# A sparse-attention and feed-forward kernel: the local heads' scores and values brought into one visit a tile, and the x tile split in two buffers

## The chip, the cores and the metric

The kernel runs on one core of a Trainium2 chip. The metric is the device time of one execution in microseconds (us); the runs of one kernel are summed up by their median. The engines are named as the profile names them: PE is the tensor engine (PEld its loading of weights), DVE the vector engine, ACT the scalar engine, POOL the GpSimd engine, SP the engine that issues DMA transfers.

## What is computed

q, k and v have 8 batches, 8 heads, 576 positions and 64 channels. Four heads of each batch are local (a query sees the 32 positions up to itself), four are strided (a query sees the earlier positions of its own residue modulo 32). The attention's output, 4608 tokens of 512 channels, goes through a feed-forward layer with an exact gelu, 512 to 2048 to 512.

```python
rel = pos[:, None] - pos[None, :]
mask_local = (rel >= 0) & (rel < stride)
mask_strided = (rel >= 0) & (pos[None, :] % stride == pos[:, None] % stride)
scores = np.where(masks[None], scale * np.matmul(q, k.transpose(0, 1, 3, 2)), -1e9)
attn = softmax(scores)                      # max taken off, 1e-9 added to the sum
x = np.matmul(attn, v).transpose(0, 2, 1, 3).reshape(B * S, H * D)
h = x @ w_in
out = (0.5 * h * (1.0 + erf(h / sqrt(2)))) @ w_out
```

## The kernel before

**The feed-forward part** sets the frame. The 4608 tokens are cut into 12 tiles of TT = 384, the 2048 hidden channels into NF = 16 blocks of 128: 192 steps, n = 16 t + f. A float32 product is made of three products of shorter floats (high with high, low with high, high with low), so every matrix is kept as a high and a low part. Step n holds, on PE, the group H(n) (`ffn_h`: 4 chunks of 128 channels x 3 products = 12 matmuls of 384 columns, L602 to L604, into one of two H banks), then the group O(n-2) (`ffn_o`: 3 blocks of 128 tokens x 3 products = 9 matmuls of 512 columns, L641 to L643). Between them ACT makes the gelu in the bank (L611) and its high part gh (L613), and DVE takes the difference gl (L615), the last to read the bank; `ffn_o` needs both. The bank of H(n) is written again by H(n+2).

**The x tile** of a token tile t is what the H groups read: high and low part, four chunks of 128 channels by 384 tokens each (`x_tile`, two tiles alive). Chunks 0 and 1 are local heads, 2 and 3 strided ones. Whoever fills it copies the high part on ACT (L230) and subtracts for the low part on DVE (L232), by `to_x`.

**Strided heads** run on DVE alone, off PE, but for the first tile: products of q and k with a sum (L477, a multiply with a reduction and the reading of its accumulator), an exponential on ACT (L487), multiply-adds with v (L517 for the first, L519 for the rest), a transpose (L527), then `to_x`. They are spread over the steps by a running cost (`run_strided`).

**Local heads** come as 36 jobs of P = 128 tokens, three to a tile (JPT = 3). A job (`band_job`) has seven parts, separated by `yield`: part 0 the scores on PE (L290, 32 matmuls of 64 columns in two banks S0 and S1, which the three jobs of a tile share, 128 columns each), part 1 mask and maximum on DVE (L304), part 2 the exponentials on ACT (L308), part 3 normalising and transposing on DVE (L311 to L314) and DMA transfers of the result into a banded buffer, part 4 the values on PE (L328, 16 matmuls of 64 columns), parts 5 and 6 `to_x`. The jobs of tiles 0 and 1 run in the kernel's start, a list of jobs written out by hand (START), which also holds steps 0 to 15. From tile 2 on, `visit(n)` puts the parts 0 of a tile's three jobs at step 16 (t-1) + 2 and their parts 4 at step 16 (t-1) + 12, each in front of that step's H group; `softmaxes(n)` places the parts between.

**Order.** ACT's and PE's instructions stand in the order in which the program is written (`manual_schedule`); from step 16 on DVE, SP and POOL are ordered by the framework's scheduler. In the start all but POOL are in the written order. In names such as H_140, gl_140 or O_8_2 the number is the step, or the tile and its token block; X_L27 is the bank of job 27's values.

## Time and profile before

| | us |
|---|---|
| median of three runs | 885.03 (884.91 to 885.48) |
| the profiled execution | 885.1 |
| its span in the trace | 883.2 |
| PE busy | 858.5 (97%) |
| DVE busy | 716.7 (81%) |
| ACT busy | 492.7 (56%) |

The span runs from the first to the last instruction; 1.9 us of the profiled execution lie around it. The busy times are shares of a span that holds a start (some 110 us, in which weights are split and the first jobs run) and a long steady part; what a wait costs has to be read in its own place. In the timeline each line is a run of like instructions with its start and duration; matmuls are pipelined, so one starts before the end of the one ahead, and the distance of two starts is what counts.

### The profile page before, as it was taken

To read this page: it belongs to the slowest core of one execution; us is meant where nothing else is said; L and a number is where in the kernel's file an instruction comes from. 1 tells how busy PE (TensorE), PEld (TensorE's weight loads), DVE (VectorE), ACT (ScalarE), POOL (GpSimd) and SP (SyncE) were. 2 spreads that over 40 slices of the span, in tenths; PEclk is the share of its full clock that TensorE was granted. 3 is DMA by queue.
4 is the path that set the end of the run, shared out by engine and by line. 5 is a ranking of instruction groups with operands and counts; after the bars stand their busy time and mean duration, and the time that the engine had idled before them with its cause. 6 is when DMAs were issued, how large, how long until landed. Compare 5 with 4: busy or idle time off the path is not lost.

```text
span 883.2 us, 19381 instructions
## 1 busy us (share of the span) xinstructions
PE 858.5 (97%) x5984; PEld 769.2 (87%) x5984; DVE 716.7 (81%) x4897; ACT 492.7 (56%) x1003; POOL 17.9 (2%) x89
## 2 busy tenths in 40 slices
PE   4599999999999999999999999999999999999998
PEld 3488899989989889889898988998988998989997
DVE  5999999988898998898999978998789897752111
ACT  5999576358447347357636536636642743643222
POOL 5000100000000000000000000000000000000000
PEclk7599999999999999999999999999999999999999
DMA  9981420230220122112113022113012102000001
GB/s 304 348 350 56 149 82 15 86 102 23 85 81 14 62 69 77 36 42 75 58 32 109 18 75 82 21 55 127 17 57 82 49 25 63 11 11 1 36 1 36
DMA packets 34551, 66.66 MB, mean 75 GB/s; under 512 B 6800, under 2 KB 16528, under 8 KB 32400
## 3 DMA queue, kind: packets, MB, share of 16 engines
q1 hardware_dynamic: 34448, 65.43, 22.7%
q8 instruction: 47, 0.77, 0.4%
q14 instruction: 56, 0.46, 0.2%
HBM read 51.64 MB, written 9.44 MB: 69 GB/s over the span
## 4 chain that ended last, share of the span: by engine, by line
PE 93%; DVE 3%; DMA 2%; SPq 1%; issue 1%; ACT 1%; DVEq 0%
PE H L602 15%; PE O L642 15%; PE O L643 15%; PE H L604 15%; PE H L603 15%; PE O L641 15%; PE X_L L328 2%; DMA vl<-in_vl_dram 2%; PE S_L L290 1%; DVE ws L153 1%; DVE w L163 1%; DVE ws L155 1%; ACT ws L151 0%; SPq L132 0%; DVE xl L424 0%
## 5 line engine op out<-in xcount | busy, mean ns | idle before, releaser
L611 ACT ACTIVATE H<-H 128x384 f32<-128x384 f32 x192 | 91.5, 477 | 334.6 <-PE H L604 295.6
L602 PE MATMUL H<-xh,w 128*128 128x384 f32 x768 | 262.4, 342 | 2.6 <-ACT xh L230 1.2
L604 PE MATMUL H<-xh,w 128*128 128x384 f32 x768 | 260.3, 339 | 1.6 <-DVE w L163 1.6
L603 PE MATMUL H<-xl,w 128*128 128x384 f32 x768 | 259.2, 338 | 0.2 <-DVE xl L232 0.2
L519 DVE SCALAR_TENSOR_TENSOR acc<-sv,sc,acc 128x64 f32<-128x64 f32 x1158 | 250.2, 281 | 0.6
L643 PE MATMUL O<-w,gl 128*128 128x512 f32 x576 | 227.9, 396 | 0.0
L642 PE MATMUL O<-w,gh 128*128 128x512 f32 x576 | 227.5, 395 | 0.0
L641 PE MATMUL O<-w,gh 128*128 128x512 f32 x576 | 224.2, 389 | 0.0
L477 DVE CUSTOM_DVE_ANT_0 junk<-sq,sk 128x64 f32<-128x64 f32 x1290 | 206.2, 221 | 1.8 <-DMA sk<-in_ks_dram 1.8
L615 DVE TENSOR_TENSOR gl<-H,gh 128x384 fp32r<-128x384 f32 x192 | 106.3, 554 | 107.8 <-ACT gh L613 107.4
L602 PEld LDWEIGHTS H<-xh,w 128*128 128x128 f32 x768 | 145.2, 189 | 12.5 <-ACT xh L230 1.4
L603 PEld LDWEIGHTS H<-xl,w 128*128 128x128 f32 x768 | 145.1, 189 | 7.9 <-DVE xl L232 0.6
L604 PEld LDWEIGHTS H<-xh,w 128*128 128x128 f32 x768 | 145.0, 189 | 2.0 <-DVE w L163 1.9
L643 PEld LDWEIGHTS O<-w,gl 128*128 128x128 f32 x576 | 108.0, 187 | 23.0
L642 PEld LDWEIGHTS O<-w,gh 128*128 128x128 f32 x576 | 108.0, 187 | 18.2
L641 PEld LDWEIGHTS O<-w,gh 128*128 128x128 f32 x576 | 108.2, 188 | 17.4
L477 DVE DVE_READ_ACCUMULATOR2_ANT sc<- 128x1 f32 x1290 | 109.3, 85 | 0.0
L613 ACT CAST gh<-H 128x384 fp32r<-128x384 f32 x192 | 92.3, 481 | 6.0
L611 ACT ACT_TABLE_LOAD x61 | 78.3, 1283 | 1.1
L487 ACT ACT_TABLE_LOAD x35 | 44.9, 1283 | 0.6
L308 ACT ACTIVATE PT_L<-P_L,nm_L 128x64 f32<-128x64 f32 x132 | 44.3, 336 | 0.3
L308 ACT ACT_TABLE_LOAD x25 | 32.1, 1283 | 2.7 <-DMA band<-PT_L 2.2
(106 smaller groups left out, 512.0 us busy)
## 6 DMA issues: line engine op xcount, KB each, us to landing
ws<-in_w_dram SPq DMA_DIRECT2D x16, 1024.0 KB, 11.4
qk<-in_qk_dram SPq DMA_DIRECT2D x36, 320.0 KB, 4.7
out_dram<-ob SPq DMA_DIRECT2D x34, 256.0 KB, 2.5
vl<-in_vl_dram SPq DMA_DIRECT2D x36, 192.0 KB, 3.4
sk<-in_ks_dram SPq DMA_DIRECT2D x8, 576.0 KB, 4.9
sv<-in_vs_dram SPq DMA_DIRECT2D x8, 576.0 KB, 3.7
band<-PT_L SPq DMA_DIRECT2D x240, 16.0 KB, 1.8
sq<-in_qs_dram SPq DMA_DIRECT2D x4, 576.0 KB, 3.8
```

Source lines behind the costliest of these rows:

```text
L308: nc.scalar.activation(pv[:, :, h, :], p1[:, h * 2 * QB:(h + 1) * 2 * QB].rearrange("p (c t) -> p c t", c=2), AF.Exp, bias=nm[:, h:h + 1], ...
L477: nc.vector.tensor_tensor_reduce(junk, sq[vi, "q"][:, r0 + r, :], sq[vi, "k"][:, c, :], 1.0, 0.0, ALU.mult, ALU.add, ss[u][:, r, c:c + 1])
L519: nc.vector.scalar_tensor_tensor(acc[:, r, :], sq[vi, "v"][:, c, :], wgt, acc[:, r, :], ALU.mult, ALU.add)
L602: nc.tensor.matmul(hp, w1[f][:, 0, c, :], xh[:, c, :], start=(c == 0), stop=False)
L603: nc.tensor.matmul(hp, w1[f][:, 0, c, :], xl[:, c, :], start=False, stop=False)
L604: nc.tensor.matmul(hp, w1[f][:, 1, c, :], xh[:, c, :], start=False, stop=(c == NC - 1))
L611: nc.scalar.activation(hp, hp, AF.Gelu)
L613: nc.scalar.copy(gh, hp)
L615: nc.vector.tensor_tensor(gl, hp, gh.bitcast(F32), ALU.subtract)
L641: nc.tensor.matmul(o, gh[:, sl], w2[f][:, 0, :], start=(f == 0), stop=False)
L642: nc.tensor.matmul(o, gh[:, sl], w2[f][:, 1, :], start=False, stop=False)
L643: nc.tensor.matmul(o, gl[:, sl], w2[f][:, 0, :], start=False, stop=(f == NF - 1))
```

## The change

- The x tile is two tiles: the local chunks as [128, 3 jobs, 2 chunks, 128 tokens], the strided ones as [128, 2 chunks, 384 tokens]. `ffn_h` reads a local chunk in three pieces of 128 columns, one for each job; the bank that it writes stays one run of 384.
- The values of tile t and the scores of tile t+1 stand in one visit, at step 16 (t-1) + 13 for t = 2 to 11; the scores of tile 2 alone stand at step 18. That makes 11 visits: one of scores, nine of both, one of values.
- Parts 1, 2 and 3 of job i lie 1, 2 and 3 steps behind the visit plus 4 i (2 i for tile 2); before, part 1 of all three jobs lay in the visit's step, and parts 2 and 3 one and two steps behind it plus 2 i.
- The values of jobs 0 and 1 stand side by side in bank X and go into x by one `to_x` of 512 columns; job 2's go into the last 128 columns of the banks S0 and S1 that the next tile's scores take, and leave by two `to_x` of 128.
- The load of the next q and k (`load_jq`) is issued behind part 0 instead of behind part 6.

The diff:

```diff
--- before.py
+++ after.py
@@ -168,8 +168,10 @@
     xt = {}
 
     def x_tile(t):
+
         if t not in xt:
-            xt[t] = [xpool.tile([P, NC, TT], F32R, name=f"x{i}_{t}", tag=f"x{i}{t % 2}") for i in "hl"]
+            xt[t] = ([xpool.tile([P, JPT, N2, P], F32R, name=f"x{i}_{t}", tag=f"x{i}{t % 2}") for i in "hl"],
+                     [xpool.tile([P, NC - N2, TT], F32R, name=f"xs{i}_{t}", tag=f"xs{i}{t % 2}") for i in "hl"])
         return xt[t]
 
 
@@ -266,9 +268,11 @@
         if x >= JPT:
             load_jv(x + 3)
         yield
-        t, c0 = divmod(x * P, TT)
-        dst = [a[:, 0:N2, c0:c0 + P] for a in x_tile(t)]
+        dst = [d[:, x % JPT] for d in x_tile(x // JPT)[0]]
         yield from to_x(*dst, xv)
+
+    def score_banks(t):
+        return [ps_a.tile([P, DM], F32, name=f"S{j}_{t}", tag=f"S{j}") for j in range(2)]
 
     def band_job(x, bt, sx=None):
 
@@ -276,10 +280,8 @@
 
         QB = STRIDE
         i = x % JPT if sx is not None else 0
-        sx = {} if sx is None else sx
-        if i == 0:
-            sx["s"] = [ps_a.tile([P, DM], F32, name=f"S{j}_L{x}", tag=f"S{j}") for j in range(2)]
-        s = [t[:, i * P:(i + 1) * P] for t in sx["s"]]
+        sx = {x // JPT: score_banks(x // JPT)} if sx is None else sx
+        s = [t[:, i * P:(i + 1) * P] for t in sx[x // JPT]]
         qv = jq[x][:, 0:2 * N2 * LU].rearrange("p (r a t) -> p r a t", r=N2, a=2)
         kv = jq.pop(x)[:, 2 * N2 * LU:].rearrange("p (r a t) -> p r a t", r=N2, a=2)
         head = [(h % 2, slice(h // 2 * 2 * QB, (h // 2 + 1) * 2 * QB)) for h in range(HL)]
@@ -318,21 +320,34 @@
                 kb = g % 2 + c
                 nc.sync.dma_start(bt[kb * QB:(kb + 1) * QB, g, :], tv[g * QB:(g + 1) * QB, c, :])
         yield
-        if i % 2 == 0:
-            sx["x"] = ps_a.tile([P, DM], F32, name=f"X_L{x}", tag="X" if i == 0 else "S0")
-        xv = sx["x"][:, i % 2 * N2 * P:(i % 2 + 1) * N2 * P].rearrange("p (r q) -> p r q", r=N2)
+        if i == 0:
+            sx["x"] = ps_a.tile([P, DM], F32, name=f"X_L{x}", tag="X")
+
+        xv = [sx["x"][:, (N2 * i + r) * P:(N2 * i + r + 1) * P] if i < 2 else sx[x // JPT + 1][r][:, JPT * P:]
+              for r in range(N2)]
         bv = bt.rearrange("p (a b) (h q) -> p a b h q", a=2, h=HL)
         for r in range(N2):
             for a in range(2):
                 for j in range(2):
-                    nc.tensor.matmul(xv[rows(j), r, a * LU:(a + 1) * LU], jv[x][:, a, 2 * r + j, :],
+                    nc.tensor.matmul(xv[r][rows(j), a * LU:(a + 1) * LU], jv[x][:, a, 2 * r + j, :],
                                      bv[:LK, a, :, 2 * r + j, :], start=True, stop=True)
         jv.pop(x)
         load_jv(x + 3)
         yield
-        t, c0 = divmod(x * P, TT)
-        dst = [d[:, 0:N2, c0:c0 + P] for d in x_tile(t)]
-        yield from to_x(*dst, xv)
+        dst = x_tile(x // JPT)[0]
+        k = x % JPT
+        if i == 0 and sx.get("two"):
+            parts = []
+        elif i == 2:
+            parts = [to_x(*[d[:, k, r] for d in dst], xv[r]) for r in range(N2)]
+        else:
+            parts = [to_x(*[d[:, k - i:k + 1].rearrange("p i r q -> p (i r q)") for d in dst],
+                          sx["x"][:, 0:(i + 1) * N2 * P])]
+        for p in parts:
+            next(p)
+        yield
+        for p in parts:
+            next(p, None)
 
 
     ka = {}
@@ -413,7 +428,7 @@
                         nc.tensor.matmul(xv[b][h * 32:(h + 1) * 32, c, :], pts[kr, c, h * 32:h * 32 + 32],
                                          vv[kr, c, h, :], start=True, stop=True, tile_position=(b * 32, h * 32))
             yield
-        xd = [x[:, N2:].rearrange("p e (m c b) -> b p c e m", c=NGR // 4, b=4) for x in x_tile(t)]
+        xd = [x.rearrange("p e (m c b) -> b p c e m", c=NGR // 4, b=4) for x in x_tile(t)[1]]
         for b in range(4):
             nc.vector.transpose(xs[:, b].rearrange("p c e m -> p (c e m)"), xv[b].rearrange("p c d -> p (c d)"))
         yield
@@ -528,8 +543,8 @@
                                 acc.rearrange("p t d -> p (t d)"))
 
             def split():
-                dst = [x[:, N2:N2 + DH, 32 * k:32 * (k + nr)].rearrange("p e (t r) -> p e t r", r=32)
-                       for x in x_tile(t)]
+                dst = [x[:, :, 32 * k:32 * (k + nr)].rearrange("p e (t r) -> p e t r", r=32)
+                       for x in x_tile(t)[1]]
                 return to_x(*dst, xs.rearrange("p t e r -> p e t r"))
             splits.append((t, split, u))
         ops.append((0.6, fin))
@@ -596,12 +611,16 @@
 
     def ffn_h(n):
         t, f = divmod(n, NF)
-        xh, xl = xt[t]
+        loc, strided_ = xt[t]
         hp = ps_h.tile([P, TT], F32, name=f"H_{n}", tag="H")
         for c in range(NC):
-            nc.tensor.matmul(hp, w1[f][:, 0, c, :], xh[:, c, :], start=(c == 0), stop=False)
-            nc.tensor.matmul(hp, w1[f][:, 0, c, :], xl[:, c, :], start=False, stop=False)
-            nc.tensor.matmul(hp, w1[f][:, 1, c, :], xh[:, c, :], start=False, stop=(c == NC - 1))
+            if c < N2:
+                o, (xh, xl) = hp.rearrange("p (i q) -> p i q", i=JPT), [x[:, :, c, :] for x in loc]
+            else:
+                o, (xh, xl) = hp, [x[:, c - N2, :] for x in strided_]
+            nc.tensor.matmul(o, w1[f][:, 0, c, :], xh, start=(c == 0), stop=False)
+            nc.tensor.matmul(o, w1[f][:, 0, c, :], xl, start=False, stop=False)
+            nc.tensor.matmul(o, w1[f][:, 1, c, :], xh, start=False, stop=(c == NC - 1))
         hps[n] = hp
 
     def ffn_g(n):
@@ -768,10 +787,15 @@
 
 
 
-    SCORES, VALUES = 2, 12
-    score_at = {ready[t - 1] + SCORES: t for t in range(2, NTILE)}
-    value_at = {ready[t - 1] + VALUES: t for t in range(2, NTILE)}
-    banks = {}
+    FIRST, VISIT = 2, 13
+    value_at = {ready[t - 1] + VISIT: t for t in range(2, NTILE)}
+    score_at = {ready[1] + FIRST: 2, **{n: t + 1 for n, t in value_at.items()}}
+    soft_at = {}
+    for n, t in score_at.items():
+        for i in range(JPT):
+            for p in (1, 2, 3):
+                soft_at.setdefault(n + p + i * (2 if t == 2 else 4), []).append((t * JPT + i, p))
+    banks = {"two": True}
     local = {}
     band = slot("band", [P, 4 * DM])
     nc.gpsimd.memset(band, 0.0)
@@ -785,28 +809,30 @@
                 local[x] = [band_job(x, bts[x % NBT], banks), 0]
             assert local[x][1] == p
             local[x][1] += 1
-            if next(local[x][0], True) is not None:
+            next(local[x][0], None)
+            if p == 0:
                 load_jq(x + 3)
 
     def visit(n):
 
-        for at, p in ((score_at, 0), (value_at, 4)):
-            for i in range(JPT if n in at else 0):
-                part(at[n] * JPT + i, p)
+        t = value_at.get(n, 0)
+        if n in score_at:
+            banks[score_at[n]] = score_banks(score_at[n])
+        for i in range(JPT if t else 0):
+            part(t * JPT + i, 4)
+        for i in range(JPT if score_at.get(n, NTILE) < NTILE else 0):
+            part(score_at[n] * JPT + i, 0)
 
     def softmaxes(n):
 
-        for i in range(JPT if n in value_at else 0):
-            part(value_at[n] * JPT + i, 5, 6)
-        for i in range(JPT if n in score_at else 0):
-            part(score_at[n] * JPT + i, 1)
-        for i in range(JPT):
-            for d, p in ((1, 2), (2, 3)):
-                t = score_at.get(n - 2 * i - d)
-                if t is not None:
-                    if p == 2:
-                        flush_exps(NU)
-                    part(t * JPT + i, p)
+        t = value_at.get(n, 0)
+        for i in range(JPT if t else 0):
+            part(t * JPT + i, 5, 6)
+        for x, p in soft_at.get(n, ()):
+            if x < NJ:
+                if p == 2:
+                    flush_exps(NU)
+                part(x, p)
 
     def step(n):
 
```

On PE, the value visit of tile 9 (jobs 27 to 29), before: between O(137) and H(140) there stand values alone.

```order
L642 MATMUL O_8_2_9117<-w_9_1000,gh_137_9538 128x512
L643 MATMUL O_8_2_9117<-w_9_1000,gl_137_9539 128x512
L328 MATMUL X_L27_9694<-band_1485,vl_27_8597 64x64 x8
L328 MATMUL X_L27_9694<-band_1485,vl_28_8607 64x64 x8
L328 MATMUL X_L29_9715<-band_1485,vl_29_8618 64x64 x8
L602 MATMUL H_140_9726<-xh_8_7858,w_12_1084 128x384
L603 MATMUL H_140_9726<-xl_8_7859,w_12_1084 128x384
```

The scores of tile 10 (jobs 30 to 32) end six steps on, in front of H(146):

```order
L290 MATMUL S0_L30_10057<-qk_32_9754 32x64
L290 MATMUL S1_L30_10058<-qk_32_9754 32x64
L602 MATMUL H_146_10107<-xh_9_8882,w_2_644 128x384
L603 MATMUL H_146_10107<-xl_9_8883,w_2_644 128x384
L604 MATMUL H_146_10107<-xh_9_8882,w_2_644 128x384
```

After, the same values stand one step later, in front of H(141), and the scores follow on them (96 instructions, of which the first two are shown; the last is followed by H(141)):

```order
L662 MATMUL O_8_2_9143<-w_10_760,gl_138_9601 128x512
L332 MATMUL X_L27_9758<-band_1489,vl_27_8678 64x64 x8
L332 MATMUL X_L27_9758<-band_1489,vl_28_8688 64x64 x8
L332 MATMUL S0_10_9756<-band_1489,vl_29_8698 64x64 x4
L332 MATMUL S1_10_9757<-band_1489,vl_29_8698 64x64 x4
L292 MATMUL S0_10_9756<-qk_30_8716 32x64
L292 MATMUL S1_10_9757<-qk_30_8716 32x64
```

In front of H(146) nothing is left but the step's own groups:

```order
L661 MATMUL O_8_2_9143<-w_15_1188,gh_143_9955 128x512
L662 MATMUL O_8_2_9143<-w_15_1188,gl_143_9956 128x512
L621 MATMUL H_146_10152<-xh_9_8962,w_2_646 128x384
L622 MATMUL H_146_10152<-xl_9_8963,w_2_646 128x384
L623 MATMUL H_146_10152<-xh_9_8962,w_2_646 128x384
```

The values went from step 140 to 141 and the scores from 146 to 141, job 29's values into S0 and S1.

On DVE, the place of the subtractions of job 29 and of gl_141, before. acc and xs belong to unit 33 of the strided heads, z and sc to unit 34, junk to unit 36:

```order
L519 SCALAR_TENSOR_TENSOR acc_33_9679<-sv_9_8656,sc_33_9217,acc_33_9679 128x64
L232 TENSOR_TENSOR xl_9_8883<-X_L29_9715,xh_9_8882 128x2x128
L503 TENSOR_REDUCE z_34_120<-sc_34_9589 128x4
L519 SCALAR_TENSOR_TENSOR acc_33_9679<-sv_9_8656,sc_33_9217,acc_33_9679 128x64
L509 TENSOR_SCALAR z_34_120<-z_34_120 128x4
L527 STREAM_TRANSPOSE xs_33_9926<-acc_33_9679 128x256
L510 RECIPROCAL z_34_120<-z_34_120 128x4
L477 ISA junk_36_0_0_10272,sc_36_10270<-sq_10_9496,sk_10_9498 128x64
L477 ISA sc_36_10270 128x1
L477 ISA junk_36_1_0_10274,sc_36_10270<-sq_10_9496,sk_10_9498 128x64
L477 ISA sc_36_10270 128x1
L615 TENSOR_TENSOR gl_141_9795<-H_141_9781,gh_141_9794 128x384
```

After, behind gl_140; the gl that follows is gl_141, behind 31 pairs of junk and sc, of which the first stands here, and four first products and four multiply-adds among these:

```order
L634 TENSOR_TENSOR gl_140_9727<-H_140_9713,gh_140_9726 128x384
L534 SCALAR_TENSOR_TENSOR acc_33_9698<-sv_9_8630,sc_33_9243,acc_33_9698 128x64
L518 TENSOR_REDUCE z_34_120<-sc_34_9608 128x4
L534 SCALAR_TENSOR_TENSOR acc_33_9698<-sv_9_8630,sc_33_9243,acc_33_9698 128x64 x4
L524 TENSOR_SCALAR z_34_120<-z_34_120 128x4
L534 SCALAR_TENSOR_TENSOR acc_33_9698<-sv_9_8630,sc_33_9243,acc_33_9698 128x64 x4
L525 RECIPROCAL z_34_120<-z_34_120 128x4
L534 SCALAR_TENSOR_TENSOR acc_33_9698<-sv_9_8630,sc_33_9243,acc_33_9698 128x64 x3
L522 TENSOR_TENSOR sc_34_9608<-sc_34_9608,z_34_120 128x4x8
L534 SCALAR_TENSOR_TENSOR acc_33_9698<-sv_9_8630,sc_33_9243,acc_33_9698 128x64 x5
L542 STREAM_TRANSPOSE xs_33_10019<-acc_33_9698 128x256
L492 ISA junk_36_0_0_10299,sc_36_10297<-sq_10_9515,sk_10_9517 128x64
```

The subtractions of the local heads moved behind gl_141, and work of the strided heads that stood behind gl_141 moved ahead of it.

## Rows read from the trace of the kernel before

**Rows 1.** The page, parts 1 and 2: busy time; granted clock of PE in 40 slices.

```profile
...
PE 858.5 (97%) x5984; PEld 769.2 (87%) x5984; DVE 716.7 (81%) x4897; ACT 492.7 (56%) x1003; POOL 17.9 (2%) x89
...
PEclk7599999999999999999999999999999999999999
...
```

**Rows 2.** Waits of PE: engine, line, releaser; us in total, times, longest.

```profile
...
PE H L602 <- DVE gl L615: 0.3, 1, 0.3
...
```

**Rows 3.** Timeline of PE, a step without a visit; start, duration, instruction.

```profile
...
303.07 0.39 PE L641 MATMUL O<-w,gh 128*128 128x512 f32 x1
...
304.92 0.39 PE L643 MATMUL O<-w,gl 128*128 128x512 f32 x1
305.15 0.33 PE L602 MATMUL H<-xh,w 128*128 128x384 f32 x1
305.32 0.34 PE L603 MATMUL H<-xl,w 128*128 128x384 f32 x1
...
307.26 0.39 PE L641 MATMUL O<-w,gh 128*128 128x512 f32 x1
...
```

**Rows 4.** Timeline of PE at the value visit of step 60.

```profile
...
298.99 0.40 PE L643 MATMUL O<-w,gl 128*128 128x512 f32 x1
299.31 1.62 PE L328 MATMUL X_L<-band,vl 96*64 96x64 f32 x48
300.86 0.44 PE L602 MATMUL H<-xh,w 128*128 128x384 f32 x1
301.14 0.33 PE L603 MATMUL H<-xl,w 128*128 128x384 f32 x1
...
```

**Rows 5.** Timeline of PE at the score visit of step 66.

```profile
...
325.85 0.40 PE L643 MATMUL O<-w,gl 128*128 128x512 f32 x1
326.18 1.17 PE L290 MATMUL S_L<-qk 64*32 64x64 f32 x96
...
327.56 0.34 PE L603 MATMUL H<-xl,w 128*128 128x384 f32 x1
...
```

**Rows 6.** Timeline of PE in the start, values followed by scores.

```profile
...
53.39 1.01 PE L328 MATMUL X_L<-first,vl 96*64 96x64 f32 x16
54.34 0.46 PE L290 MATMUL S_L<-qk 64*32 64x64 f32 x32
...
```

**Rows 7.** Timeline of PE, last matmul of H(139) and H(140), first of H(142).

```profile
...
647.25 0.33 PE L604 MATMUL H<-xh,w 128*128 128x384 f32 x1
...
653.18 0.33 PE L604 MATMUL H<-xh,w 128*128 128x384 f32 x1
...
659.62 0.33 PE L602 MATMUL H<-xh,w 128*128 128x384 f32 x1
...
```

**Rows 8.** Timeline of DVE around steps 138 to 141.

```profile
...
642.79 0.74 DVE L517 TENSOR_SCALAR acc<-sv,sc 128x64 f32<-128x64 f32 x4
...
649.60 0.54 DVE L615 TENSOR_TENSOR gl<-H,gh 128x384 fp32r<-128x384 f32 x1
...
650.46 4.98 DVE L519 SCALAR_TENSOR_TENSOR acc<-sv,sc,acc 128x64 f32<-128x64 f32 x25
655.37 0.54 DVE L615 TENSOR_TENSOR gl<-H,gh 128x384 fp32r<-128x384 f32 x1
...
659.10 0.45 DVE L527 STREAM_TRANSPOSE xs<-acc 128x256 f32<-128x256 f32 x1
...
```

**Rows 9.** Timeline of DVE around steps 91 to 93.

```profile
...
443.91 0.23 DVE L477 CUSTOM_DVE_ANT_0 junk<-sq,sk 128x64 f32<-128x64 f32 x1 [1.60 <-DMA sk<-in_ks_dram]
...
444.06 0.22 DVE L477 CUSTOM_DVE_ANT_0 junk<-sq,sk 128x64 f32<-128x64 f32 x1
...
452.98 0.56 DVE L615 TENSOR_TENSOR gl<-H,gh 128x384 fp32r<-128x384 f32 x1
...
```

**Rows 10.** Timeline of PE, first matmul of H(95).

```profile
...
453.70 0.34 PE L602 MATMUL H<-xh,w 128*128 128x384 f32 x1
...
```

**Rows 11.** Waits of DVE, columns as in rows 2.

```profile
...
DVE gl L615 <- ACT gh L613: 107.4, 45, 5.4
...
```

## The prediction

> **What bounds the kernel now.** I read the page first, then the waits of the tensor engine (PE), then its timeline around the visits of the local heads, and last the vector engine's (DVE) timeline. [...] The list of PE's waits has twelve rows; eleven name operations of the start or its first tiles, and the one on the step's last operation, gl, is 0.3 us in all [rows 2]; it lies at 55 us, in the start too. After the start PE waits for nothing: a step without a visit takes 4.19 us, 303.07 to 307.26, and inside it the way from the last matmul of an O group (L643) to the second matmul of the next H group (L603) takes 0.40 us [rows 3]. That 0.40 is the unbroken passage against which I price a visit.
>
> A **value visit** (48 matmuls, L328) stands in that passage and stretches it from 298.99 to 301.14, 2.15 us: it costs 1.75 [rows 4]. A **score visit** (96 matmuls, L290) stretches it from 325.85 to 327.56, 1.71 us: 1.31 [rows 5]. Ten tiles pay both: 10 x 3.06 = 30.6 us. The ends of a visit are the part that a merge can save: 0.32 us pass between the start of the last L643 and that of the visit's first matmul (298.99 to 299.31), where unbroken the next matmul comes after 0.23 (304.92 to 305.15), and on the way out the first H matmul holds the second up for 0.28 (300.86 to 301.14) instead of 0.17. That is about 0.2 us a visit; the rest is the matmuls themselves, which stay.
>
> **The change, part by part.** *Merging.* Values of tile t and scores of t+1 now stand in one visit: nine merged ones (steps 29, 45, ..., 157), one of scores alone (18) and one of values alone (173): 11 visits for 20. I build a merged one from rows: 0.32 entry; 1.55 of values, from L328's start to the start of what follows (299.31 to 300.86) [rows 4]; then scores from their start to the first L603, 1.38 (326.18 to 327.56) [rows 5]; less 0.40: 2.85. The open piece is the step from values to scores, which do not adjoin in the steady part of this trace. They do once in the start: there L328 starts at 53.39 and lasts 1.01, and L290 starts at 54.34, 0.06 before that modelled end [rows 6]; H after L328 starts 0.07 before it as well (300.86 against 299.31 + 1.62) [rows 4]. So going from values to scores costs what going from values to H cost, and my sum stands: 3.06 - 2.85 = 0.20 saved, x 9 = **1.8 us**. Its bounds: nothing, if the inner step costs as much as both ends saved (nearest row against it: rows 6), and 9 x 0.32 = 2.9, if the whole entry goes. I take 1.8, since rows 6 show the very sequence.
>
> *The x tile in two buffers.* The six matmuls of each H group that read local heads now take the moving operand in three pieces of 128 columns that lie 256 apart; the result stays one run. 6 x 192 = 1152 matmuls, all on the path. No H matmul before reads pieces, but L328 does: its moving operand is two pieces of 32. 48 of them, 24 pairs of 2 x 64 columns, take 1.55 us, 65 ns a pair with the way out of the visit in it [rows 4]; an H matmul of 384 columns takes 0.17 (305.15 to 305.32) [rows 3], that is 57 ns for 128. What is over, 8 ns a pair, bounds what its four pieces cost; three pieces then cost 6 ns at most, 6.9 us in all. The other bound is nothing: I see no row that excludes it, and none that shows a gain from pieces. I take nothing, because the 24 x 8 = 0.19 us over are of the size of a visit's way out (0.1 us on the first H matmul alone).
>
> *Softmax parts moved.* Parts 1 to 3 of job i now lie 1 to 3 steps, plus 4 i, behind the visit; they are ACT and DVE work and no PE. Work is the same in number. The last bands are written some eleven steps after their visit, and PE reads them five steps on, over 20 us, far more than a band's DMA takes. *Copies.* Two jobs' values leave bank X by one ACT copy and one DVE subtraction of 512 columns, the third's by two of 128: three subtractions as before. They run beside H and O. *qk loads* are issued behind the visit instead of at the job's end; they are needed one tile, 70 us, later; on SP's queue they stand ahead of stores and bands that nobody awaits within four steps. *Banks.* S0 and S1 now hold job 2's values beside the next scores; both are read within some ten steps and written again after sixteen. All four at nothing; the cover is the whole steps in between, and where it were gone a wait of some microseconds would show on PE before L328, L290 or L602.
>
> *Order on DVE.* This is where something is given back. PE may start H(n+2) only when gl(n) has read the bank of H(n). I call the lag of n the time from the last matmul end of H(n) to the end of gl(n). With H(140) ending at 653.18 + 0.33 = 653.51 and H(142) starting at 659.62, the lag allowed is 6.11 [rows 7]. Seen: gl(139) ends 2.56 after its H (650.14 against 647.58), gl(140) 2.40 (655.91 against 653.51) [rows 7, 8]. The worst in the steady part that I found: some steps after a wait of 1.60 us for a DMA, gl(93) ended at 453.54 [rows 9], 0.16 before the H(95) that needed it [rows 10], a lag of 5.95. Forty-five of the 192 gl waited for ACT, so DVE had caught up there [rows 11]. The scheduler has now put more DVE work ahead of the gl of a merged visit's step. For step 141 I price its list: 21 multiply-adds at 0.196 (25 from 650.46 to 655.37), four first products and a transpose and gl at their rows less the 0.07 by which the next instruction starts early, 0.67 + 0.38 + 0.47 [rows 8], 31 reduce pairs at just under 0.15 (443.91 to 444.06) [rows 9], four small ones at some 0.14 (an estimate, below the shortest of these): 10.7 us, where PE needs 4.19 + 2.85 = 7.04 from H(140) to H(141). gl(140) has 3.8 us of work in 4.19, so its lag falls from 2.56 to 2.2; gl(141) comes to 2.2 + 10.7 - 7.0 = 5.9, and gl(142), with 4.8 of work in 4.19, to 6.5: 0.4 us over, which PE waits. Priced likewise, the nine visits' steps have 8.6, 8.9, 8.4, 7.7, 7.7, 7.9, 9.7, 10.7 and 9.0 us. From lags of 2.4 to 4 most end at 3 to 5.5, and only 30 and 142 come near the limit. I take **0.4 us** in all; the bounds are 0, and, if each visit were met with some 4.5 us of lag, halfway from rows 8 to rows 10, 0.4 to 1 us at eight or nine places, up to some 6 us.
>
> **Sum.** -1.8 + 0.4 = -1.4. The profiled execution took 885.1 us, of which 883.2 are span; the median of the runs is 885.03, the same within 0.1. 885.03 - 1.4 gives **883.6**. Two tenths of a per cent, 1.77 us, is about what a measurement here tells from no change; faster then means below 883.26, slower above 886.80.
>
> **Rivals.** *DVE becomes the bound at the merged visits.* For it: 81% busy [rows 1], the longer lists above, the 0.16 of rows 10. Against it: the 45 waits for ACT [rows 11]. Paid are 0.9 to 6 us, 884.1 to 889. It ends on the slower side from 1.8 + 1.77 = 3.6 us of waiting on, 0.4 us at each of nine visits, which takes lags some 2 us above that of step 140 where the visits begin.
>
> *H pays for three pieces.* From 3.1 ns for each of 1152 matmuls the kernel is slower by 0.2%: -1.4 + 3.6 = +2.2 (887.2); at 1.2 ns the gain is gone. For it: no H matmul here has read pieces, and they are all on the path. Against it: L328's pieces of 32 run near the rate of plain columns [rows 4]. [...]
>
> *The merge gives nothing,* since a visit's ends are paid between values and scores as well: 885.0 + 0.4 = 885.4; rows 6 speak against it. *The merge gives the whole entry:* 885.03 - 2.9 + 0.4 = 882.5.
>
> **How the numbers follow.** Forecast (the merge gains 1.8, give or take 0.4, DVE and pieces take 0 to 0.9; 882.8 to 884.2): 0.65, some two fifths of it below 883.26. DVE as the bound: 0.17, a quarter of it slower. Pieces: 0.08, most of it slower. Nothing from the merge: 0.05. The whole entry: 0.05, faster. Faster 0.27 + 0.05 = 0.32; slower 0.04 + 0.07 = 0.11, with 0.02 for what I have not seen 0.13; the same 0.55. The range runs from 882.4 to 886.2: the forecast, both cases of the merge, and DVE's part up to 3 us.
>
> **What would show it.** Right: the passage from L643 through a merged visit to L603 takes about 3.25 us at nine places, L290 starts just before L328's modelled end; a step without a visit still takes 4.19; PE's waits gain at most a row on gl of some tenths, near step 142. Wrong: a step without a visit of 4.205 or more (pieces: six a step at 3 ns), a row of several us on gl (DVE), a gap of over 0.2 us between L328 and L290 (no merge gain), or PE waiting before L328 or L290 for a band, a load or a bank.

## The result and the profile after

The changed kernel takes 886.72 us in the median of 20 runs, beside 885.00 for the kernel before in as many: a ratio of 1.0023, with a 95% interval of 1.0014 to 1.0031 (the ratios in this document lie nearer that of the means than that of the medians; the medians differ by 1.7 us, the means by 2.0). It is 0.2% slower, just short of what I had called slower (from 886.80 on). What the median doesn't say is the spread: 885.19 to 889.55 us, where the kernel before keeps to 884.88 to 885.68. The profiled execution is one of its shorter ones, 885.84 us with a span of 883.9.

The page of that execution, parts 1, 2 and 4. PE's busy time is the same as in [rows 1] but for 0.4 us. The third row gives each engine's share of the chain that ended last; DVE now holds 10% of it, where it held 3% (the fourth row, of the kernel before). These 10% are not time lost: where PE waits for a gl, the chain goes back through DVE's whole list in front of it, and only PE's wait at its end is paid.

```profile
...
PE 858.9 (97%) x5984; PEld 771.0 (87%) x5984; DVE 716.2 (81%) x4897; ACT 489.6 (55%) x1001; POOL 17.8 (2%) x89
...
PEclk9999999999999999999999999999999999999999
...
PE 85%; DVE 10%; DMA 2%; issue 1%; POOL 1%; ACT 1%; SPq 0%; POOLq 0%; DVEq 0%; ACTq 0%
...
```

```profile
...
PE 93%; DVE 3%; DMA 2%; SPq 1%; issue 1%; ACT 1%; DVEq 0%
...
```

**What was forecast on PE came.** Its timeline at the merged visit of step 141, from the last matmul of the O group to the second of the H group:

```profile
...
652.32 0.40 PE L662 MATMUL O<-w,gl 128*128 128x512 f32 x1
652.65 1.15 PE L332 MATMUL X_L<-band,vl 96*64 96x64 f32 x32
653.63 0.64 PE L332 MATMUL S<-band,vl 96*64 96x64 f32 x16
654.19 1.17 PE L292 MATMUL S<-qk 64*32 64x64 f32 x96
655.29 0.45 PE L621 MATMUL H<-xh,w 128*128 128x384 f32 x1
655.58 0.34 PE L622 MATMUL H<-xl,w 128*128 128x384 f32 x1
...
```

652.32 to 655.58 is 3.26 us, against the 3.25 put together from [rows 4, 5]; L292 starts 0.08 before the modelled end of L332, as in [rows 6]. Steps without a visit take 4.19 us as in [rows 3]; here are the O groups of two of them (672.39 to 676.58):

```profile
...
672.39 0.39 PE L660 MATMUL O<-w,gh 128*128 128x512 f32 x1
...
676.58 0.39 PE L660 MATMUL O<-w,gh 128*128 128x512 f32 x1
...
```

So the merge saves what it should, and matmuls that read three pieces cost nothing that can be seen.

**What took it back** stands in the waits of PE, where [rows 2] had 0.3 us:

```profile
...
PE H L621 <- DVE gl L634: 2.0, 3, 1.5
...
```

The row counts three waits, of which the longest is 1.5 us. With the time that PE's weight loads waited, the H groups behind steps 30, 141 and 142 start some 2.8 us late in sum (from last matmul to last matmul the distances are 4.65, 5.92 and 4.79 us instead of 4.19). The span grew by 0.7 us, so some 2.1 us must have been gained, near the 1.8 of the sum. The waits of DVE tell why gl came late; the columns are those of [rows 11]. First the kernel before, where PE waited for none of this, then the changed kernel:

```profile
...
DVE junk L477 <- DMA sk<-in_ks_dram: 1.8, 2, 1.6
...
DVE acc L517 <- DMA sv<-in_vs_dram: 0.9, 1, 0.9
...
```

```profile
...
DVE gl L634 <- ACT gh L632: 107.0, 45, 5.0
...
DVE junk L492 <- DMA sk<-in_ks_dram: 2.6, 2, 2.2
DVE acc L532 <- DMA sv<-in_vs_dram: 2.1, 2, 1.5
...
```

The longest wait for sk, 2.18 us, stands in front of gl(29), and PE loses some 0.5 us behind step 30; the longest for sv stands in front of gl(141), and PE loses 2.3 us behind steps 141 and 142.

In detail, at step 141. The timeline of PE gives the end of H(141), 657.66, and the start of the H(143) that waited:

```profile
...
657.32 0.34 PE L623 MATMUL H<-xsh,w 128*128 128x384 f32 x1
...
665.41 0.44 PE L621 MATMUL H<-xh,w 128*128 128x384 f32 x1 [1.49 <-DVE gl L634]
...
```

and that of DVE gives the instruction which held up everything behind it, among these gl(141):

```profile
...
662.20 0.74 DVE L532 TENSOR_SCALAR acc<-sv,sc 128x64 f32<-128x64 f32 x4 [1.48 <-DMA sv<-in_vs_dram]
...
664.80 0.56 DVE L634 TENSOR_TENSOR gl<-H,gh 128x384 fp32r<-128x384 f32 x1
...
```

gl(141) ends 7.70 us after H(141), not the forecast 5.9: DVE stood for 1.48 us in front of L532, the first product with v of a new group of the strided heads, until the load of sv had landed. That buffer has one copy, so its load starts when the old group's last product is done; it was issued at 656.94, and DVE had come to the new group's first product at 660.72, 3.8 us later. SP's timeline shows in what company the load starts:

```profile
...
653.37 1.29 SPq L191 DMA_DIRECT2D vl<-in_vl_dram  x3
654.77 0.84 SPq L185 DMA_DIRECT2D qk<-in_qk_dram  x2
656.94 0.33 SPq L469 DMA_DIRECT2D sv<-in_vs_dram  x1
657.36 0.38 SPq L185 DMA_DIRECT2D qk<-in_qk_dram  x1
...
```

Five loads of the local jobs were issued in the 3.6 us ahead of it and one right after. In the kernel before, sv is issued in the same step; the vl loads lie 8.8 us ahead of it, and the qk loads 18 us behind:

```profile
...
650.33 1.28 SPq L189 DMA_DIRECT2D vl<-in_vl_dram  x3
659.09 0.35 SPq L454 DMA_DIRECT2D sv<-in_vs_dram  x1
...
677.23 0.40 SPq L183 DMA_DIRECT2D qk<-in_qk_dram  x1
...
```

The DMA view of the 11 us around it, first of the changed kernel, then of the kernel before (the issue's last column is the median time from issue to landing): 2.19 MB move where 0.61 moved, and the same 576 KB take 5.2 us instead of 3.6.

```profile
...
DMA packets 914, 2.19 MB, mean 199 GB/s; under 512 B 112, under 2 KB 112, under 8 KB 912
...
sv<-in_vs_dram SPq DMA_DIRECT2D x1, 576.0 KB, 5.2
...
```

```profile
...
DMA packets 146, 0.61 MB, mean 56 GB/s; under 512 B 16, under 2 KB 16, under 8 KB 144
...
sv<-in_vs_dram SPq DMA_DIRECT2D x1, 576.0 KB, 3.6
...
```

### The profile page after: what moved, and what is told of

The parts are those of the page before. It is cut to its first block, busy times and chain, and to the rows that moved or that the text cites. A ratio compares the mean times of both kernels' runs of the same rounds, so it can differ in the third digit from the quotient of the medians.

```text
span 883.9 us, 19396 instructions
## 1 busy us (share of the span) xinstructions
PE 858.9 (97%) x5984; PEld 771.0 (87%) x5984; DVE 716.2 (81%) x4897; ACT 489.6 (55%) x1001; POOL 17.8 (2%) x89
## 4 chain that ended last, share of the span: by engine, by line
PE 85%; DVE 10%; DMA 2%; issue 1%; POOL 1%; ACT 1%; SPq 0%; POOLq 0%; DVEq 0%; ACTq 0%
PE H L621 14%; PE H L623 14%; PE O L661 14%; PE H L622 14%; PE O L662 14%; PE O L660 13%; DVE junk L492 2%; DVE acc L534 2%; PE X_L L332 1%; PE S L292 1%; DVE gl L634 1%; DMA sk<-in_ks_dram 1%; DVE ws L153 1%; DMA sv<-in_vs_dram 1%; DVE P_L L306 0%
## 5 line engine op out<-in xcount | busy, mean ns | idle before, releaser
L534 DVE SCALAR_TENSOR_TENSOR acc<-sv,sc,acc 128x64 f32<-128x64 f32 x1158 | 254.2, 286 | 0.6
L621 PE MATMUL H<-xh,w 128*128 128x384 f32 x384 | 133.1, 347 | 4.3 <-DVE gl L634 2.0
L623 PE MATMUL H<-xh,w 128*128 128x384 f32 x384 | 131.7, 343 | 1.0 <-DVE w L163 1.0
L622 PE MATMUL H<-xl,w 128*128 128x384 f32 x384 | 130.6, 340 | 0.0
L623 PE MATMUL H<-xsh,w 128*128 128x384 f32 x384 | 129.1, 336 | 0.0
L622 PE MATMUL H<-xsl,w 128*128 128x384 f32 x384 | 129.1, 336 | 0.0
L621 PE MATMUL H<-xsh,w 128*128 128x384 f32 x384 | 129.1, 336 | 0.0
L492 DVE DVE_READ_ACCUMULATOR2_ANT sc<- 128x1 f32 x1290 | 113.1, 88 | 0.0
L621 PEld LDWEIGHTS H<-xh,w 128*128 128x128 f32 x384 | 72.7, 189 | 15.2 <-DVE gl L634 3.3
L622 PEld LDWEIGHTS H<-xl,w 128*128 128x128 f32 x384 | 72.7, 189 | 7.9 <-DVE xl L234 0.4
L623 PEld LDWEIGHTS H<-xh,w 128*128 128x128 f32 x384 | 72.5, 189 | 1.5 <-DVE w L163 1.5
```

Source lines behind the costliest of these rows:

```text
L492: nc.vector.tensor_tensor_reduce(junk, sq[vi, "q"][:, r0 + r, :], sq[vi, "k"][:, c, :], 1.0, 0.0, ALU.mult, ALU.add, ss[u][:, r, c:c + 1])
L534: nc.vector.scalar_tensor_tensor(acc[:, r, :], sq[vi, "v"][:, c, :], wgt, acc[:, r, :], ALU.mult, ALU.add)
L621: nc.tensor.matmul(o, w1[f][:, 0, c, :], xh, start=(c == 0), stop=False)
L622: nc.tensor.matmul(o, w1[f][:, 0, c, :], xl, start=False, stop=False)
L623: nc.tensor.matmul(o, w1[f][:, 1, c, :], xh, start=False, stop=(c == NC - 1))
```

## The experiments

Three theories. **A:** the loads which the merged visit issues together meet the loads of sk and sv, these land later, DVE waits for them in front of a gl, and PE waits for that gl. **B:** the scheduler's order on DVE alone, 8 to 10.7 us of work ahead of a merged visit's gl, makes it late. **C:** the H matmuls pay for reading three pieces. All ratios are to the kernel before on the same chip. The expectations speak of A+B as well: the order takes the slack, and the loads decide how much is waited.

### Two parts alone

*split* leaves the merge out and keeps the rest.

```diff
-    score_at = {ready[1] + FIRST: 2, **{n: t + 1 for n, t in value_at.items()}}
+    score_at = {ready[t - 1] + FIRST: t for t in range(2, NTILE)}
...
-                soft_at.setdefault(n + p + i * (2 if t == 2 else 4), []).append((t * JPT + i, p))
+                soft_at.setdefault(n + p + i * 2, []).append((t * JPT + i, p))
```

> The changed kernel without the merge: scores at step 16 (t-1) + 2 as before, values at + 13; two x buffers, job 2's values in S0 and S1 and the copies as in the changed kernel. Ten visits of each kind, so 1.8 us more of PE than in the changed kernel. Theory A: the loads of q and k lie at position 2 again, away from sv and sk; 885.0 to 885.5 us. Theory B: DVE's lists ahead of gl are 5.5 to 7.1 us, against 5.94 us allowed plus the visit's 1.75: 885.0 to 885.5. Theory C: 888 or more, since pieces cost and nothing is saved.

885.12 us in the median, ratio 0.9998 (0.9990 to 1.0007). Steps without a visit take 4.19 us. Two x buffers, the new copies and pieces cost nothing that this interval shows: C falls. It doesn't tell A from B, which both expected this. DVE waits for sk longer than in the changed kernel, and PE never waits for it:

```profile
...
DVE junk L492 <- DMA sk<-in_ks_dram: 4.6, 2, 3.1
...
```

The late load was harmless here, since gl had room behind it. It is the merged visit's step, with its longer list, that has none.

*noload* leaves out the strided heads' loads from the third group on; DVE computes on the second group's data.

```diff
...
-        t = spool.tile([P, NR, D], F32, name=f"s{nm}_{gr}", tag=f"s{nm}", bufs=1)
+        old = kept.get(nm) if gr not in order_g[:2] else None
+        t = spool.tile([P, NR, D], F32, name=f"s{nm}_{gr}", tag=f"s{nm}", bufs=1) if old is None else old
+        kept[nm] = t
...
-            nc.sync.dma_start(t[:, o + r0:o + r1], src[b, :, r0:r1])
+            if old is None:
+                nc.sync.dma_start(t[:, o + r0:o + r1], src[b, :, r0:r1])
```

> The changed kernel, but the strided heads' loads of sq, sk and sv are left out from the third group on (they compute on the second group's data, so their part of the output is not the reference's). The order on DVE is the changed kernel's (8.0 us ahead of gl(29), 10.6 ahead of gl(141)), and DVE has no load to wait for. Theory A+B (the order takes the slack, the loads decide the waiting): PE waits for gl by 0 to 0.6 us in all; ratio 0.9980 to 0.9990, spread as the kernel before's. Theory B (order alone): 2 us or more of waiting stay, ratio 1.000 to 1.003. If merging gives nothing: 1.000 without waits.

883.08 us (882.95 to 883.57), ratio 0.9979 (0.9970 to 0.9988): 1.9 us below the kernel before, with a spread of 0.6. PE's only wait for gl is that of the start:

```profile
...
PE H L626 <- DVE gl L639: 0.5, 1, 0.5
...
```

gl(141) ends 5.86 us after its H here, against the 5.9 of my sum. PE's waits are what A+B expected. But DVE's list in front of gl(141) is not the changed kernel's, which the expectation took it to be: without the loads the scheduler orders it anew, and 12 products of q and k with 35 multiply-adds stand where 31 and 21 stood. The stretch from the end of gl(140) to that of gl(141), in the changed kernel and in *noload* (its length, then DVE's busy us and instructions, PE's granted clock, and what the DMA engines did):

```profile
...
652.82:665.35 12.53, 10.75 (x94) 1.00 0.52 175
...
```

```profile
...
652.21:662.90 10.69, 10.46 (x70) 1.00 0.46 149
...
```

Of the 12.5 us of the changed kernel 1.48 are the wait for sv. The 11.05 that are left would put gl(141) some 6.2 us behind its H and gl(142) some 6.8 (7.70 and 8.28 less 1.48, an estimate), over the 6.11 that [rows 7] allow; in *noload* they come at 5.86 and 5.75. So merging is worth 1.8 to 1.9 us, and the whole loss goes with the loads, but not all of it was waiting for them: behind step 141 a part belongs to the order. The runs below give its size. At step 29 it is the wait alone: gl(30) ended 6.43 us after its H, 2.18 of them for sk, and 3.39 here.

### The same kernel again

> The changed kernel once more, for a second profile. Theory A (loads collide): its times lie between 885.2 and 889.6 us, and what this execution takes over 883.2 us (before less 1.8) is PE waiting for gl in a few steps behind the merged visits of steps 29 and 141, where DVE stands waiting for the loads of sk and sv; where these loads land within 4.6 and 3.6 us, as in the kernel before, there is next to no wait. Theory B (order on DVE alone): the same steps wait, by the same 0.4 to 0.9 us in each execution, whatever the loads take. Theory C (pieces): steps without a visit take 4.20 us or more.

887.78 us in the median of ten, ratio 1.0023 (1.0014 to 1.0032); the profiled execution took 888.3. Its DMA view between 652 and 665 us, DVE's timeline there and PE's:

```profile
...
sv<-in_vs_dram SPq DMA_DIRECT2D x1, 576.0 KB, 6.2
...
```

```profile
...
663.79 0.74 DVE L532 TENSOR_SCALAR acc<-sv,sc 128x64 f32<-128x64 f32 x4 [2.42 <-DMA sv<-in_vs_dram]
...
```

```profile
...
667.00 0.69 PE L621 MATMUL H<-xh,w 128*128 128x384 f32 x1 [2.42 <-DVE gl L634]
...
```

The sv load took 6.2 us, DVE waited 2.42 for it, and PE as long for gl(141). That is not the whole loss. The busy times of this stretch (core, then each engine's busy us and instructions, then PE's granted clock):

```profile
...
660.00:664.00 4.00, 4.00 (x22) 3.65 (x21) 1.58 (x22) 1.12 (x3) 0.00 (x0) 1.00 0.57 206
664.00:667.00 3.00, 0.59 (x3) 0.15 (x1) 3.00 (x26) 0.00 (x0) 0.00 (x0) 0.97 0.01 3
667.00:669.00 2.00, 2.00 (x6) 2.00 (x7) 2.00 (x12) 0.00 (x0) 0.00 (x0) 0.50 0.00 0
...
671.00:675.00 4.00, 4.00 (x22) 3.67 (x21) 4.00 (x31) 3.92 (x12) 0.00 (x0) 1.00 0.00 0
...
```

After PE had worked for 0.59 us out of 3, its clock stood at 0.50 for the stretch behind, and H(143) took 3.8 us from the start of its first to the end of its last matmul, where H(142) took 2.3. The two steps from H(142) to H(144) took 12.5 us instead of 8.4, 4.1 more. The slow H(143) covers a wait that PE has behind step 142 in the other executions, so the clock's own part is smaller than 4.1 - 2.4: some 0.9 us, an estimate from the 0.8 us that are lost beside the wait for sv in the other executions (under *qklate*). In the first profile a wait of 1.5 us left the clock where it was, at 1.00. The two profiled executions differ by 2.5 us, and PE's losses behind steps 30 and 141 by 2.3. No run of 889 us was profiled; that these are of the same kind is likely, not shown.

> The changed kernel beside the three below on the same chip: 2 to 2.5 us above the kernel before in the median, with a spread of 3 us or more. Theories A and B both say so.

On the chip of the runs below: 888.77 us (885.99 to 889.24), ratio 1.0033 (1.0021 to 1.0046), 3.7 us above the kernel before in the median of five runs, where 2 to 2.5 were expected. Its profiled execution was a short one again: sv 4.9 us, gl(141) 7.38 us after H(141).

### The loads moved

*qklate* issues the loads of q and k behind part 3 of each job.

```diff
...
-            if p == 0:
-                load_jq(x + 3)
+            if p == 3:
+                load_jq(x + 3, True)
```

The new argument keeps the load in program order on SP.

> The changed kernel, with the loads of q and k issued behind part 3 of each job (3, 7 and 11 steps behind the visit) instead of at the visit; the order on DVE is all but the same. Theory A: sv lands within 3.8 us at step 141, DVE no longer waits for it (1.5 us before), PE's waits behind step 141 fall from 2.2 to 0.5 us; sk at step 28 still has the vl loads beside it and may wait. Median 884.0 to 885.3, spread of the runs below 1.5 us. Theory B: no change, 886.7 in the median, 885.2 to 889.6. Theory C: no change.

885.74 us (885.15 to 886.54), ratio 1.0004 (0.9995 to 1.0013), 2.0 us below *again* beside it. That is a little above what A alone expected, and 1 us under the median that B expected. sv at step 141 takes 3.8 us, near the 3.6 of the kernel before, and DVE waits a third as long:

```profile
...
sv<-in_vs_dram SPq DMA_DIRECT2D x1, 576.0 KB, 3.8
...
```

```profile
...
662.55 0.74 DVE L534 TENSOR_SCALAR acc<-sv,sc 128x64 f32<-128x64 f32 x4 [0.51 <-DMA sv<-in_vs_dram]
...
```

gl(141) ends 6.68 us after H(141), and PE still loses 1.4 us behind steps 141 and 142, where A expected 0.5. Over the three executions of the changed kernel, whose list ahead of gl(141) is the same, lag follows landing one for one: landing 4.9, 5.2 and 6.2 us, gl(141) 7.38, 7.70 and 8.63 us after H(141), where 6.11 is allowed. (*qklate* has 90 instructions there instead of 94.) PE's loss from H(142) to H(145), against three plain steps, holds a part that no load decides: 2.3 us beside 1.48 of DVE's wait for sv in the first profile, 2.0 beside 1.16 in *again2*, 1.4 beside 0.51 here. Some 0.8 us stay each time, whatever the load takes: that is the list's own length, theory B's part.

Two things keep *qklate* above the kernel before. At step 28 sk still landed after 7.0 us, beside the vl loads. And a late qk load was now issued 0.6 us ahead of sv in step 122; that sv took 5.0 us, DVE waited 1.73 for it, and PE lost some 1.0 behind step 125.

*loadslate* moves the loads of v as well.

```diff
...
-        load_jv(x + 3)
...
-            if p == 0:
-                load_jq(x + 3)
+            if p == 3:
+                load_jq(x + 3, True)
+                load_jv(x, True)
```

> The changed kernel, with the loads of q, k and of v issued behind part 3 of each job, away from the merged visit; the order on DVE as in the changed kernel. Theory A (loads alone): sk lands within 4.8 us at step 28 and sv within 4 at step 141, PE waits for gl at no step or for less than 0.5 us in all, 1.5 us below the kernel before (ratio 0.9983), spread below 1. Theory B (order alone): waits behind steps 29 and 141 stay at 1.5 us or more, ratio 1.000 to 1.002. Both together (A+B: the order takes the slack, the loads decide how much is waited): some 0.6 us of waiting left behind step 141, ratio 0.9985 to 0.9995.

886.19 us (885.56 to 887.35), ratio 1.0011 (1.0002 to 1.0020): a miss for A and for A+B, worse than *qklate* if anything; the ratio alone would fit B (1.000 to 1.002). At step 141 sv landed after 3.7 us, DVE waited 0.40 for it and PE lost 1.2, some 0.8 more again. Its waits of DVE say that the collisions were not removed but moved:

```profile
...
DVE acc L535 <- DMA sv<-in_vs_dram: 5.2, 4, 2.1
DVE junk L495 <- DMA sk<-in_ks_dram: 4.6, 2, 2.4
...
```

A pair of late loads now falls at position 10 of a tile, right ahead of sv at 295 and 574 us, which took 5.0 and 5.3 us instead of 3.4 and 3.9 in the changed kernel; the second makes PE wait behind step 125. And sk at step 28 was no faster, though nothing of the local jobs was issued in the 3 us before it:

```profile
...
q8 instruction: 2, 0.03, 0.9%
...
sk<-in_ks_dram SPq DMA_DIRECT2D x1, 576.0 KB, 6.9
...
```

In the same stretch of the kernel before, sk took 4.6 us. What slowed it here is open: two transfers of instructions lie in the stretch where one lay before, but no run took them away.

*visit9* puts the merged visits at position 9, where no load of sk or sv falls.

```diff
-    FIRST, VISIT = 2, 13
+    FIRST, VISIT = 1, 9
```

> The changed kernel with the merged visits at step 16 (t-1) + 9 instead of + 13, the scores of tile 2 at step 17. No load of sk or sv falls there, and the lists of DVE ahead of the gl of a visit's step are 3.5 to 4.7 us instead of 7.6 to 10.6. Theories A and B: no wait of PE for gl, 883.2 to 883.8 us, spread below 0.8. Theory C: 886.7 or more, steps without a visit above 4.20. If merging saves nothing: 885.0.

908.66 us, ratio 1.0258 (1.0244 to 1.0272), and no test of A or B: the bands of tile 2 are too close in front of their values, and PE waits for these in the first merged visit; the step with it took 20.2 us instead of 6.9, part of it at a lower granted clock (0.59 in the mean from 150 to 160 us, 0.55 from 160 to 166). In the visits of steps 41 and 121 PE stood for 3.0 and 3.3 us more, with nothing in the profile that it waited for. Steps without a visit take 4.19 us here too, so C fails once more.

```profile
...
PE S L332 <- DMA band<-PT_L: 9.6, 2, 7.6
...
```

DVE stood 7.6 us for the sk of step 25, just behind PE's long wait:

```profile
...
DVE junk L492 <- DMA sk<-in_ks_dram: 10.2, 2, 7.6
...
```

### The order on DVE

*glfirst* queues the strided work that is written in a merged visit's step behind that step's gl; the loads stay.

```diff
...
+            if n in value_at and n in score_at:
...
+                with tc.issue_after(last_gl[0].ins):
+                    run_strided(upto)
...
```

> The changed kernel, its loads where they were, but the strided heads' DVE work that is written in the step of a merged visit is queued behind that step's gl. Ahead of gl(141) stand 1.4 us instead of 10.6; ahead of gl(29) 8.5 as before, since that work is written a step earlier. Theory A alone: no change from the changed kernel (ratio 1.002). Theory B or A+B: no wait behind step 141, whatever sv's load takes; behind step 29 the wait stays (0.7 to 1.7 us, since sk is still late); ratio 0.999 to 1.000, spread below 1.5 us.

897.64 us, ratio 1.0142 (1.0128 to 1.0156). The forecast for the two places came: no wait behind step 141, and the old one behind step 29. The work put off came due elsewhere: in steps 82 and 162 a tile's last strided work came so late that ACT stood over 6 us for its transposes, its copies ob of O waited behind that, and PE waited for ob, 3.5 and 4.4 us. These two steps took 9.1 and 10.3 us.

```profile
...
PE O L661 <- ACT ob L668: 7.8, 2, 4.4
...
PE H L622 <- DVE gl L635: 1.3, 3, 0.7
...
```

*best* adds the loads of *loadslate* to it.

> Both edits: loads away from the visit and the visit step's strided work behind gl. Theories A, B and A+B: no wait of PE for gl after the start, 1.6 to 1.8 us below the kernel before (ratio 0.9980 to 0.9985), spread as that of the kernel before (0.8 to 1.3 us). If merging itself saves nothing: ratio 1.000.

901.21 us, ratio 1.0180 (1.0166 to 1.0194): the same fault, and 3.6 us more. Putting gl first by hand shows that the order has a part in the wait at 141; as a mend it costs more than it gives.

### DVE given its data earlier

*halves* cuts the strided heads' loads into the first six rows and the rest.

```diff
...
-            nc.sync.dma_start(t[:, o + r0:o + r1], src[b, :, r0:r1])
...
+            m = min(r1, r0 + EARLY)
+            r0, r1 = {None: (r0, r1), 0: (r0, m), 1: (m, r1)}[half]
+            if r0 < r1:
+                nc.sync.dma_start(t[:, o + r0:o + r1], src[b, :, r0:r1])
```

> The changed kernel, with the strided heads' loads of q, k and v each cut into the first six rows and the rest, first rows first; order on DVE and place of the other loads unchanged. DVE can begin on six rows. Theory A+B: DVE's waits for sk at step 29 and sv at step 141 fall by 1 to 2 us, PE's wait for gl to under 1 us; ratio 0.9985 to 0.9998, spread below 1.5 us. Theory B: no change, 1.002 to 1.003.

885.85 us (885.01 to 887.74), ratio 1.0011 (1.0002 to 1.0019): less than half of the way that A+B expected. The first rows of sv still travel with five loads of the local jobs, took 4.4 us and made DVE wait at step 141:

```profile
...
661.98 0.74 DVE L538 TENSOR_SCALAR acc<-sv,sc 128x64 f32<-128x64 f32 x4 [1.82 <-DMA sv<-in_vs_dram]
...
```

*halveslate* is *halves* with the loads of q and k behind part 3, as in *qklate*.

> The same, and the loads of q and k for the local jobs behind part 3 of each job. Theory A+B: like halves or 0.3 us better, ratio 0.9980 to 0.9995. Theory B: 1.002 to 1.003.

884.38 us (883.87 to 884.92), ratio 0.9992 (0.9983 to 1.0001). At step 141 DVE waits 0.28 us, and PE by 1.0 in three waits, two of them of 0.4 to 0.5 us behind steps 141 and 142 (and one of 0.5 in the start), where I had forecast one of 0.4; 0.28 of waiting and 1.0 us lost from H(142) to H(145) again leave some 0.8 for the order:

```profile
...
PE H L629 <- DVE gl L642: 1.0, 3, 0.5
...
```

*final* has the loads cut, and issues all six loads of the local jobs together behind part 3 of a tile's first job, three steps behind the visit.

```diff
...
-        load_jv(x + 3)
...
-            if p == 0:
-                load_jq(x + 3)
+            if p == 3 and x % JPT == 0:
+                for y in range(x, x + JPT):
+                    load_jv(y, True)
+                for y in range(x, x + JPT):
+                    load_jq(y + 3, True)
```

> The changed kernel, with the strided heads' loads cut in six rows and the rest, and all loads of the local jobs (v for the coming visit, q and k for the one after) issued behind part 3 of a tile's first job, three steps behind the merged visit, where no load of sk or sv is due; order on DVE as in the changed kernel. Theory A+B: sk at step 28 and sv at step 141 land their first rows within 3.5 us, DVE waits for them by under 1 us, PE waits for gl by 0.5 to 1 us behind step 141 and nowhere else; ratio 0.9978 to 0.9992, clearly faster than the kernel before. If loads of the local jobs were not what makes sk and sv late: ratio 0.9990 to 1.0010 as with the halves alone.

884.50 us (884.02 to 885.37), ratio 0.9992 (0.9982 to 1.0001), at the edge of what A+B expected, not clearly faster than the kernel before, and inside the range of the rival as well (0.9990 to 1.0010, the loads of the local jobs not to blame). What speaks against the rival is the trace: sv's first rows land after 2.3 us at step 141, 4.4 in *halves*, and gl(141) ends at 6.36. PE loses 0.9 us behind steps 141 and 142, with 0.18 of DVE's wait, and nothing behind step 30. DVE still waits at step 28 for sk, with no load of the local jobs in its window, by 1.9 us:

```profile
...
DVE junk L501 <- DMA sk<-in_ks_dram: 2.6, 2, 1.9
...
```

So both mended kernels lie about 2.3 us below the changed kernel, each measured against the kernel before. In the median both lie 0.6 us below the kernel before, which the intervals don't set apart from nothing, and *noload* lies 1.3 lower still; some 0.8 of that is the order's part behind step 141, by the rows above. A second copy of the strided heads' buffers would let their loads start earlier; it was not tried.

## Why the prediction was wrong

It said 883.6 us, 882.4 to 886.2, and gave "the same" 0.55; 886.72 lies outside the range. That it still counts as the same, 0.08 short of slower, is no merit of the forecast: a gain that came and a loss that was not foreseen nearly met.

- **Bound and visits: right.** PE's row of work decides (busy for 97% in both profiles); the merged passage took 3.26 us for 3.25, and *noload* measures the whole saving at 1.9 for 1.8.
- **Pieces: right.** I took nothing out of a bound of 0 to 6.9 us; *split* shows nothing.
- **"qk loads ... All four at nothing": the step that failed.** I asked by when the moved loads are needed, and found 70 us; I didn't ask which transfers they would meet. I had read that they pass stores and bands on SP's queue, but not that sq, sk and sv are issued from the same queue and can be awaited within 4 to 5 us, though [rows 9] show DVE waiting 1.60 us for sk. The loads of q and k went from position 2 of a tile to position 13, beside those of v; the trace of before has sk or sv issued there in steps 29, 45 and 141. At 141 this took sv from 3.6 to 5.2 us, and 1.5 of the 2.8 us that PE lost are the wait for it; with the q and k loads elsewhere it took 3.8. At 45 sk took 7.3 us instead of 4.4, and DVE wasn't there yet. At 29 sk took 6.3 instead of 4.6, but with the loads moved it stayed at 6.9 to 7.0, so this part, some 0.5 us, isn't shown to be theirs.
- **Order on DVE: the mechanism right, the sum short.** The limit of 6.11 us held, and the list's work too: 10.75 us busy for the 10.7. The list was summed as work alone. It holds 0.2 us of waiting for ACT and 1.48 for sv, and gl(141), put at 5.9, came at 7.70, some 6.2 without sv's wait. So the order's own part is some 0.8 us where I had 0.4, and the waits for sk and sv, put at nothing, make it 2.8 in one execution and more in another. Of the two steps that "come near the limit", 142 does so by its list; 30 does so by DVE's wait of 2.18 us for sk alone.
- **The rival "DVE becomes the bound at the merged visits"** is the case that came, inside its 884.1 to 889, at 0.17. Its place was right, its price too; I had it come from lags at the beginning of the visits, and these were as forecast (2.18 at step 140). It came from loads inside the list. A range that took in this rival whole would have held the time; I cut it at 3 us of loss.
- **The clock** was in none of the cases: behind the wait of 2.42 us PE ran at half the rate for some 3 us (a granted clock of 0.50).

## What to carry to other kernels

When a change gathers work in one place, list every transfer that it issues there, and every transfer that others await there: a load that is not needed for 70 us can still delay one that is needed in 4 (here sv at step 141, from 3.6 to 5.2 us). Merging visits of an engine takes slack away from whoever feeds it (here gl(141) came 3.85 us after its H in the kernel before and 7.70 after the merge, 5.86 without the loads); price the waits inside the other engine's list, from the longest that the trace shows for each, and not its work alone. And where a scheduler sets the order, a kernel with something left out may have another order: compare the lists before a difference is put down to what was left out. And where a kernel's times spread after a change though its instructions are fixed, look for a wait that follows a transfer's length (here sv, 4.9 to 6.2 us).

## What the runs showed of the hardware

- **A wait was paid again in the clock.** In *again* PE stood for 2.42 us, worked 0.59 us out of 3, and then ran for some 3 us at a granted clock of 0.50: 12 matmuls in 3.8 us for 2.3. Behind the wait of 1.49 us in the first profile the clock stayed at 1.00, and so it did behind the 3.33 us of *visit9* at step 121, where PE worked 0.67 us out of 4. In these three the length of the wait alone doesn't tell.
- **Landing times of one load in one program differed** from execution to execution: sv at step 141 took 5.2, 6.2 and 4.9 us in the profiled executions of the changed kernel (the first, *again* and *again2*), with the same loads issued around it. The row of that window below, in 40 slices of 0.28 us, stands at 263 to 384 GB/s from the 20th slice to the 33rd, while the loads overlapped, 332 in the mean. The load of sv alone, in the kernel before, stands at 385 to 402 in its three highest slices (second row, 657 to 668 us). So up to five loads together moved no more than one alone at its height (332 GB/s in the mean against 385 to 402), and the 576 KB of sv took 5.2 us among them, 3.6 alone. Why the same set takes longer in one execution than in another stays open. The DMA views of the changed kernel's first profile, 652 to 663 us, and of the kernel before:

```profile
...
GB/s 0 0 0 0 0 0 0 0 74 141 246 402 387 194 186 246 244 246 214 322 384 378 331 328 315 263 264 361 335 335 343 357 339 242 199 101 93 56 28 0
...
```

```profile
...
GB/s 0 0 0 0 0 0 60 0 0 0 0 184 268 218 201 402 385 385 101 0 0 0 0 0 0 30 0 0 0 0 0 0 0 0 0 0 0 0 0 0
...
```

- The scores followed the values without a gap that the trace can show: at step 141 of the changed kernel L292 starts 0.08 us before the modelled end of L332, as H does behind the values, by 0.07 [rows 4].
